# A recurrence and a highway layer on one core: shared PSUM slots, 4 KB load runs and a new instruction list

## The chip, the cores and the metric

The kernel runs on one core of a Trainium2 chip. The metric is the device time in microseconds (us), the median of several runs. Names used below: PE is the matrix engine (TensorE), DVE is VectorE, ACT is ScalarE, POOL is GpSimd, and SP is the engine that here issues all large transfers. SBUF is the on-chip memory, PSUM the small memory (eight banks of 2 KB in each of 128 partitions) that PE writes its results to.

## The reference

Two stages, one after the other. A gated recurrence runs over 6336 steps for 4 sequences with 256 channels, and then a highway layer is applied to each of the 25344 results:

```python
# x, f_logit: (4, 6336, 256); lower_bound: (256,)
sig = 1 / (1 + exp(-f_logit))
f = lower_bound + (1 - lower_bound) * sig
for t in range(S):
    h = f[:, t] * h + (1 - f[:, t]) * x[:, t]
    y[:, t] = h
# highway layer, w_h and w_t: (256, 256)
H = maximum(y @ w_h, 0)
T = 1 / (1 + exp(-(y @ w_t + b_t)))
out = T * H + (1 - T) * y
```

The types outside are float32. In all, 51.9 MB are read as x and f_logit and 25.95 MB are written.

## The kernel before

The tokens are cut into 24 units of 1024 tokens (8 blocks of 128, all of one sequence) and one last unit that holds the remaining 192 tokens of each of the 4 sequences (8 blocks of 96). The work on a unit before and in the recurrence is called its front, the highway layer its back. The first three units have their fronts cut into pieces, and the last unit has both cut in two, so there are 30 front pieces and 26 back pieces. Tokens lie on partitions when they are loaded; PE transposes them, so that the recurrence runs along the free dimension, with channels on partitions, as one scan instruction on VectorE for each half of the 256 channels.

Each step has a letter:

- L, X: load f_logit (tile lt) and x (tile xt) of a piece. Q: load the weights.
- U: ScalarE, u = sigmoid(-f_logit). P: GpSimd, bv = u * x for two blocks.
- A: PE transposes u into PSUM (uT). F: ScalarE, f = 1 - (1 - lb) * u out of uT.
- B: PE transposes bv into PSUM (bT). S: VectorE, the scan y out of f and bT.
- G, Z: PE, the two products with the weights (gp and zp), from y.
- T: ScalarE, t = sigmoid(zp + b). D: VectorE, d from y and gp (the ReLU and the subtraction of y in one instruction).
- E, H: e = d * t, the first part of the columns on VectorE (E) and the rest on GpSimd (H).
- O: PE, op = y + e, transposed back to tokens, four blocks in one PSUM tile. C, V: copy op to SBUF on ScalarE (C) or VectorE (V). R: store.

A string of letters gives the order in which all of these are put into the program. Each engine serves its own instructions strictly in that order.

```python
BUFS = dict(lt=5, xt=5, o=8, u=4, bv=2, f=6, t=2, d=2, e=2, y=7)
...
def load(i, name, src):
    u, j0, j1 = fronts[i]
    np_ = units[u][0]
    t = fs[i][name] = new(name, [NB, D], FP32)
    pin(nc.sync.dma_start(pairs(t[:np_, :j1 - j0]), tokens(src, u, j0, j1, 2)))   # runs of 2 tokens = 2 KB
...
def gpsimd_mul(out_, a, b):
    ins = pin(nc.gpsimd.tensor_mul(out_, a, b))
    while port:                     # GpSimd waits for the last e of VectorE that stands before it
        tc.add_manual_dep(ins.ins, port.pop().ins.name, ...)
...
def psum(piece, m, s, key, dtype):
    t = ps1.tile([P, NB * P], dtype, tag=key, name=key)     # one slot for each of uT, bT, zp, gp
    for c, h in enumerate(halves(piece)[m]):
        s[key, h] = t[:, c * 512:c * 512 + width(piece)]
        yield s[key, h], h
...
def scan(i, h):
    ...
        pin(nc.vector.tensor_tensor_scan(y, fs[i]["f", h][:, c:c + w], fs[i]["bT", h][:, c:c + w],
                                         0.0 if prev is None else prev, op0=ALU.mult, op1=ALU.add))
...
SHARE = 448                         # columns of e, for each half, that GpSimd takes
...
def e_dve(j):
    port.append(pin(nc.vector.tensor_mul(*e_cols(j, 0, width(backs[j]) - shared(j)))))
def e_pool(j):
    gpsimd_mul(*e_cols(j, width(backs[j]) - shared(j), width(backs[j])))

QB = NB // 2
def o_pe(j, q):
    op = bs[j]["op", q] = ps1.tile([P, QB, D], FP32, tag="op", name="op")       # one slot for op
    ...
            pin(nc.tensor.matmul(o, y[:, h, cols], diag[:, h], start=True, stop=False))
            pin(nc.tensor.matmul(o, bs[j]["e"][:, h, cols], ident_b, start=False, stop=True))

def copied(j, q):                   # in the last three pieces (HELPED) ScalarE and VectorE share the copy
    g = min(QB, shape(backs[j])[1] - q * QB)
    return g, g // 2 if j >= len(backs) - HELPED else g
...
PLAN = (
    "XLLXLXQQLXUUAPFFBAPSSUFFBASSWLLXLXPFFUPBAPFFUUPWSSLLXXLXPPGABZPPFFTDSSGABZUFFTDSSEAGBZFUFUTHPPPPPPDS"
    ... [cut] ...
    "OGFCTAOESDPHPPUCBZGOSDFTCBAZGORRRXRRRRXPHPUFTCSDEBAGZOSDFFTCABZGOFTCPPHRRRSSDEZGOBTFCRDGOZHSDDESCROT"
    "TCEVRGZOTTCDDVROEVCROCVR"
)
for k in PLAN:
    kinds[k][0](*next(todo[k]))
```

The PSUM slots before: uT and bT one bank each, zp, gp and op two banks each, one slot for each name, eight banks in all.

Of the kernel before, what the change touches and what calls it, by code (L numbers as in the profile page):

```python
# [19 lines left out]
def kernel(  # L20
# [43 lines left out]

    HELPED = 3

    first = ctx.enter_context(tc.tile_pool(name="first", bufs=1))
# [14 lines left out]
    def pin(ins):  # L84
        return tc.keep_in_program_order(ins)

    def pairs(t):

        return t.rearrange("p (k j) d -> p k (j d)", j=2)

    def inner(t):

        return t.rearrange("p k d j -> p k j d")
# [1 line left out]
    def tokens(src, u, j0, j1, j):  # L95

        np_, _, b, per, a = units[u]
        if per == NB:
            return src[b, a + j0 * np_:a + j1 * np_, :].rearrange("(k p j) d -> p k (j d)", p=np_, j=j)
        return src[b + j0 // per:b + j1 // per, a:a + per * np_, :].rearrange("b (p j) d -> p b (j d)", j=per)  # L100

    def load(i, name, src):
        u, j0, j1 = fronts[i]
        np_ = units[u][0]
        t = fs[i][name] = new(name, [NB, D], FP32)
        pin(nc.sync.dma_start(pairs(t[:np_, :j1 - j0]), tokens(src, u, j0, j1, 2)))

    def shape(piece):

# [43 lines left out]
    def gpsimd_mul(out_, a, b):  # L153

        ins = pin(nc.gpsimd.tensor_mul(out_, a, b))  # L155
        while port:
            tc.add_manual_dep(ins.ins, port.pop().ins.name, mybir.DependencyInfo(
                mybir.DependencyClass.Sync, mybir.DependencyReason.DATA), reason="shared port")

    def product(i, k):  # L160
        np_, _ = shape(fronts[i])
        if k == 0:
            fs[i]["bv"] = new("bv", [NB // 2, D, 2], BF16)
        gpsimd_mul(inner(fs[i]["bv"][:np_, k:k + 1])[:, 0], fs[i]["u"][:np_, 2 * k:2 * k + 2],
                   fs[i]["xt"][:np_, 2 * k:2 * k + 2])

    def width(piece):
        np_, nb = shape(piece)
# [3 lines left out]

        return ((0,), (1,)) if width(piece) > 512 else ((0, 1),)

    def psum(piece, m, s, key, dtype):

        t = ps1.tile([P, NB * P], dtype, tag=key, name=key)
        for c, h in enumerate(halves(piece)[m]):
            s[key, h] = t[:, c * 512:c * 512 + width(piece)]
            yield s[key, h], h  # L180

    def decay_pe(i, m):
        np_, nb = shape(fronts[i])
        for uT, h in psum(fronts[i], m, fs[i], "uT", FP16):
            for j in range(nb):
                pin(nc.tensor.transpose(uT[:, j * np_:(j + 1) * np_], fs[i]["u"][:np_, j, h * P:(h + 1) * P],  # L186
                                        ident_h[:np_, :np_]))

    def decay_act(i, h):

        np_, N = shape(fronts[i])[0], width(fronts[i])
        f = fs[i]["f", h] = new("f", [NB * P], FP16)
        pin(nc.scalar.activation(f[:, :N].rearrange("p (k q j) -> p k q j", q=np_, j=2),  # L193
                                 fs[i]["uT", h].rearrange("p (k j q) -> p k q j", q=np_, j=2), AF.Identity,
                                 scale=ncc[:, h:h + 1], bias=1.0))

    def b_pe(i, m):
        np_, nb = shape(fronts[i])
        for bT, h in psum(fronts[i], m, fs[i], "bT", BF16):

            for k in range(nb // 2):
                pin(nc.tensor.transpose(bT[:, 2 * k * np_:2 * (k + 1) * np_].bitcast(FP32),  # L202
                                        fs[i]["bv"][:np_, k, h * P:(h + 1) * P].rearrange("p d j -> p (d j)").bitcast(FP32),
                                        ident_f[:np_, :np_]))

# [17 lines left out]
        u, j0, j1 = backs[j]  # L223
        return ys[u][:, :, j0 * units[u][0]:j1 * units[u][0]]

    def ffn_pe(j, m, key, k):
        N = width(backs[j])
        for p, h in psum(backs[j], m, bs[j], key, FP32):
            for ki in range(NH):
                for a in range(0, N, 512):  # L230
                    e = min(a + 512, N)
                    pin(nc.tensor.matmul(p[:, a:e], w_sb[:, k, ki, h * P:(h + 1) * P], y_of(j)[:, ki, a:e],  # L232
                                         start=ki == 0, stop=ki == NH - 1))
# [9 lines left out]
        pin(nc.vector.scalar_tensor_tensor(bs[j]["d"][:, m, :width(backs[j])], y_of(j)[:, m], ncc[:, m:m + 1],  # L243
                                           bs[j]["gp", m], op0=ALU.mult, op1=ALU.max))

    SHARE = 448

    def shared(j):

# [5 lines left out]
        return (bs[j][key][:, :, a:e] for key in "edt")  # L255

    def e_dve(j):
        port.append(pin(nc.vector.tensor_mul(*e_cols(j, 0, width(backs[j]) - shared(j)))))  # L258

    def e_pool(j):  # L260
        gpsimd_mul(*e_cols(j, width(backs[j]) - shared(j), width(backs[j])))

    QB = NB // 2

    def o_pe(j, q):

        op = bs[j]["op", q] = ps1.tile([P, QB, D], FP32, tag="op", name="op")
        (np_, nb), y = shape(backs[j]), y_of(j)
        j0, j1 = q * QB, min((q + 1) * QB, nb)
        g = min(j1 - j0, units[backs[j][0]][3])  # L270
        for k in range(j0, j1):
            b, i = divmod(k - j0, g)
            cols = slice((j0 + b * g) * np_ + i, (j0 + (b + 1) * g) * np_, g)
            for h in range(NH):
                o = op[:np_, k - j0, h * P:(h + 1) * P]
                pin(nc.tensor.matmul(o, y[:, h, cols], diag[:, h], start=True, stop=False))  # L276
                pin(nc.tensor.matmul(o, bs[j]["e"][:, h, cols], ident_b, start=False, stop=True))  # L277

    def copied(j, q):

        g = min(QB, shape(backs[j])[1] - q * QB)
        return g, g // 2 if j >= len(backs) - HELPED else g

    def o_copy(j, q, engine):
        np_ = shape(backs[j])[0]
        if ("o", q) not in bs[j]:
            bs[j]["o", q] = new("o", [QB, D], FP32)
        g, a = copied(j, q)
        part = slice(0, a) if engine is nc.scalar else slice(a, g)
        copy = nc.scalar.copy if engine is nc.scalar else nc.vector.tensor_copy  # L290
        pin(copy(bs[j]["o", q][:np_, part], bs[j]["op", q][:np_, part]))  # L291

    def store(j, q):
        u, j0, _ = backs[j]
        a, (g, _) = j0 + q * QB, copied(j, q)
        per = min(g, units[u][3])
        pin(nc.sync.dma_start(tokens(out_bsd, u, a, a + g, per),
                              bs[j]["o", q][:units[u][0], :g].rearrange("p (k j) d -> p k (j d)", j=per)))

    def each(pieces, count):  # L300
        return [(i, k) for i, piece in enumerate(pieces) for k in range(count(piece))]

    def groups(piece):
        return -(-shape(piece)[1] // QB)


    kinds = {
# [1 line left out]
        "X": (lambda i, _: load(i, "xt", x), each(fronts, lambda p: 1)),  # L309
        "Q": (lambda i, k: load_weights(k), [(0, 0), (0, 1)]),  # L310
        "U": (lambda i, _: gate(i), each(fronts, lambda p: 1)),
        "P": (product, each(fronts, lambda p: shape(p)[1] // 2)),
        "A": (decay_pe, each(fronts, lambda p: len(halves(p)))),
        "F": (decay_act, each(fronts, lambda p: NH)),
        "B": (b_pe, each(fronts, lambda p: len(halves(p)))),
        "S": (scan, each(fronts, lambda p: NH)),
        "W": (lambda i, h: weights(h), [(0, 0), (0, 1)]),
        "Z": (lambda j, m: ffn_pe(j, m, "zp", 1), each(backs, lambda p: len(halves(p)))),
        "T": (t_act, each(backs, lambda p: NH)),
        "G": (lambda j, m: ffn_pe(j, m, "gp", 0), each(backs, lambda p: len(halves(p)))),  # L320
        "D": (d_dve, each(backs, lambda p: NH)),
        "E": (lambda j, _: e_dve(j), each(backs, lambda p: 1)),
        "H": (lambda j, _: e_pool(j), [(j, 0) for j in range(len(backs)) if shared(j)]),
        "O": (o_pe, each(backs, groups)),
        "C": (lambda j, q: o_copy(j, q, nc.scalar), each(backs, groups)),
        "V": (lambda j, q: o_copy(j, q, nc.vector), [p for p in each(backs, groups) if p[0] >= len(backs) - HELPED]),
        "R": (store, each(backs, groups)),
    }

    PLAN = (  # L330
        "XLLXLXQQLXUUAPFFBAPSSUFFBASSWLLXLXPFFUPBAPFFUUPWSSLLXXLXPPGABZPPFFTDSSGABZUFFTDSSEAGBZFUFUTHPPPPPPDS"
        "SOGABZCFTDSSAOGHPPPPFABZDSUFCTGBZALLXLXXLLRUTUFDSBGEESDOZBAGCTUFSDPPPPHZOBASTCFGZOBAPPPPHTCFDSZGOABD"
        "ESTUCFGZOABTFCDZAGOHPPPPFTCSDEEAGBOZXXRRLRRRRLLXFUCTDSAGBOZDSPHPPPFCTAOBZGESDFCOBATUFPPPPHPPZGATFCSD"
        "BZGAOTFCUSDPPHBZGAOXRRXXLRXLRRRTFCSDEBGAZOFTCESDABZGOPPPPPPHFTUCSDABGZOSEDPPHFTCABZGOFTUCSDRRXLLXRRR"
        "XBZGAOSDTFCBAGOZPHPPPPSDEFUTCBAGZOSDFTCABZGOPPHPPSDEFTCXLLRRRRBGAOZESDUFCTBOAGZSPHPPPPPPUFTCBADSGZOB"
        "FTCDESAGOZBHPPPPUCFTDSOGAZBCTFDSOGZBAHPCTUFDEESGZOABXRRRXRLLXLLRRDSTFCPPPPPHZGAOBTFCDSZGOBAUTCDSPPPH"
        "ZGODEFTCUBZAGOFTCESDABZGOFTCUSDPPHPPHPPPABZGOSDRXRRLRRRLXTCFBZOAGSEDTCFBZAGOTUCFSDBZGOAPPPPPHTCSDEZB"
        "OGFCTAOESDPHPPUCBZGOSDFTCBAZGORRRXRRRRXPHPUFTCSDEBAGZOSDFFTCABZGOFTCPPHRRRSSDEZGOBTFCRDGOZHSDDESCROT"
        "TCEVRGZOTTCDDVROEVCROCVR"
    )  # L340
    assert all(PLAN.count(k) == len(places) for k, (_, places) in kinds.items())
    todo = {k: iter(places) for k, (_, places) in kinds.items()}
    for k in PLAN:
        kinds[k][0](*next(todo[k]))
# [1 line left out]
_INS = ['x', 'f_logit', 'lower_bound', 'moe_w_h', 'moe_w_t', 'moe_b_t']  # L346
_OUTS = [((25344, 256), 'float32')]
# [25 lines left out]
```

## Time and profile before

| | |
|---|---|
| time, median of 3 runs | 219.93 us (219.38 to 220.0) |
| span of the profiled run | 219.6 us |
| a scan of 1024 columns (S), VectorE | 2340 ns, x40 |
| d (D), 1024 columns, VectorE | 1259 ns, x48 |
| e (E), 1152 elements, VectorE | 839 ns mean, x24 |
| e (H), 896 elements, GpSimd | 1911 ns, x24 |
| bv (P), 512 elements, GpSimd | 1173 ns, x96 |
| f, t, o copy (F, T, C), 1024 columns, ScalarE | 1176, 1165, 1060 ns |
| u (U), 2048 elements, ScalarE | 1955 ns, x21 |
| bytes moved | 78.68 MB, mean 358 GB/s over the span |

A page of the profile begins with the busy time of each engine and its share of the span. The durations of one instruction in the table overlap a little with the next one on the same engine, so the time from start to start in the timeline is shorter (2.26 us for a scan that is shown with 2.34). The chain that ended last follows the run back from its last instruction, at each step to what released it. A wait is listed with the engine and tile that waited, what it waited for, the total in us, the number of times and the longest.

### The profile page before, as it was taken

To read this page: it belongs to the slowest core of one execution; us is meant where nothing else is said; L and a number is where in the kernel's file an instruction comes from. 1 tells how busy PE (TensorE), PEld (TensorE's weight loads), DVE (VectorE), ACT (ScalarE), POOL (GpSimd) and SP (SyncE) were. 2 spreads that over 40 slices of the span, in tenths; PEclk is the share of its full clock that TensorE was granted. 3 is DMA by queue.
4 is the path that set the end of the run, shared out by engine and by line. 5 is a ranking of instruction groups with operands and counts; after the bars stand their busy time and mean duration, and the time that the engine had idled before them with its cause. 6 is when DMAs were issued, how large, how long until landed. Compare 5 with 4: busy or idle time off the path is not lost.

```text
span 219.6 us, 4569 instructions
## 1 busy us (share of the span) xinstructions
PE 188.4 (86%) x1772; PEld 132.9 (61%) x1800; DVE 197.2 (90%) x154; ACT 195.4 (89%) x194; POOL 161.1 (73%) x136
## 2 busy tenths in 40 slices
PE   0578787799999999999998999999999969998840
PEld 0435554466776766776766677566767656766640
DVE  1488978999999999999999999999999997999931
ACT  3679999999999999999999999999999958987621
POOL 4758579699769697889986979599687769663200
PEclk9999999999999999999999999999999997999975
DMA  5999999999999999999999999999999992644553
GB/s 146 401 408 408 411 403 408 409 404 409 405 416 415 403 414 404 411 417 409 409 410 407 402 418 416 409 408 406 416 413 413 349 357 112 215 169 168 212 213 103
DMA packets 34741, 78.68 MB, mean 358 GB/s; under 512 B 2336, under 2 KB 2848, under 8 KB 34720
## 3 DMA queue, kind: packets, MB, share of 16 engines
q1 hardware_dynamic: 34176, 78.39, 92.1%
q8 instruction: 14, 0.23, 0.4%
q10 hardware_dynamic: 544, 0.00, 0.1%
q14 instruction: 7, 0.06, 0.1%
HBM read 52.43 MB, written 25.95 MB: 357 GB/s over the span
## 4 chain that ended last, share of the span: by engine, by line
PE 29%; DVE 25%; DMA 15%; ACT 14%; issue 9%; POOL 4%; SPq 1%; DVEq 0%; POOLq 0%; ACTq 0%
DVE y L217 13%; PE gp L232 9%; DMA xt<-in_x_dram 9%; DVE d L243 8%; PE zp L232 6%; DMA lt<-in_f_logit_dram 5%; ACT t L238 5%; ACT f L193 4%; ACT o L291 4%; PE bT L202 4%; PE op L276 4%; PE op L277 3%; PE uT L186 3%; POOL bv L155 3%; DVE e L258 2%
## 5 line engine op out<-in xcount | busy, mean ns | idle before, releaser
L155 POOL TENSOR_TENSOR bv<-u,xt 128x512 bf16<-128x512 f16 (+1 forms) x100 | 114.3, 1173 | 30.8 <-DVE e L258 8.7
L217 DVE TENSOR_TENSOR_SCAN y<-f,y,bT 128x1024 bf16<-128x1024 f16 (+3 forms) x56 | 106.7, 1919 | 2.1 <-PE bT L202 2.0
L243 DVE SCALAR_TENSOR_TENSOR d<-y,ncc,gp 128x1024 bf16<-128x1024 bf16 (+1 forms) x52 | 62.7, 1209 | 3.0 <-PE gp L232 2.9
L193 ACT ACTIVATE f<-uT,ncc 128x1024 f16<-128x1024 f16 (+3 forms) x60 | 59.7, 1007 | 2.3 <-PE uT L186 2.3
L291 ACT COPY o<-op 128x1024 f32<-128x1024 f32 (+2 forms) x50 | 51.1, 1021 | 10.8 <-PE op L277 8.1
L238 ACT ACTIVATE t<-zp,bt 128x1024 bf16<-128x1024 f32 (+1 forms) x52 | 58.0, 1120 | 1.9 <-PE zp L232 1.0
L232 PEld LDWEIGHTS <-w_sb 128*128 128x128 f16 x400 | 38.2, 99 | 35.3 <-issue 4.4
L276 PE MATMUL op<-diag,y 128*128 128x128 f16 (+1 forms) x400 | 51.6, 222 | 3.5 <-ACT o L291 1.8
L155 POOL TENSOR_TENSOR e<-d,t 128x896 bf16<-128x896 bf16 x24 | 45.9, 1911 | 11.8 <-DVE e L258 5.0
L232 PE MATMUL gp<-y,w_sb 128*128 128x512 bf16 (+1 forms) x189 | 51.8, 387 | 2.9 <-DVE d L243 1.5
L277 PE MATMUL op<-ident_b,e 128*128 128x128 bf16 (+1 forms) x400 | 51.6, 222 | 2.5 <-POOL e L155 2.2
L149 ACT ACTIVATE u<-lt 128x2048 f16<-128x2048 f32 (+3 forms) x30 | 49.6, 1657 | 3.3 <-DMA lt<-in_f_logit_dram 3.1
L277 PEld LDWEIGHTS <-e 128*128 128x128 bf16 (+1 forms) x400 | 45.5, 116 | 10.6 <-issue 3.3
L232 PE MATMUL zp<-y,w_sb 128*128 128x512 bf16 (+1 forms) x183 | 49.5, 377 | 0.9
L276 PEld LDWEIGHTS <-y 128*128 128x128 bf16 (+1 forms) x400 | 45.7, 116 | 3.9
L186 PE MATMUL uT<-ident_h,u 128*128 128x128 f16 (+1 forms) x400 | 32.5, 227 | 8.6 <-ACT u L149 6.8
L202 PE MATMUL bT<-ident_f,bv 128*128 128x128 f32 (+1 forms) x200 | 32.4, 284 | 7.5 <-DVE y L217 5.9
L186 PEld LDWEIGHTS <-u 128*128 128x128 f16 (+1 forms) x400 | 27.5, 102 | 16.6 <-ACT u L149 8.2
L202 PEld LDWEIGHTS bT<-ident_f,bv 128*128 128x128 f32 (+1 forms) x200 | 22.0, 144 | 14.9 <-issue 5.5
L258 DVE TENSOR_TENSOR e<-d,t 128x1152 bf16<-128x1152 bf16 (+1 forms) x26 | 20.7, 817 | 0.5 <-ACT t L238 0.5
L217 DVE TENSOR_TENSOR_SCAN y<-f,bT 128x512 bf16<-128x512 f16 (+2 forms) x8 | 10.5, 1341 | 3.6 <-PE bT L202 3.6
L291 DVE COPY o<-op 128x512 f32<-128x512 f32 (+1 forms) x4 | 2.8, 690 | 4.8 <-DMA out_dram<-o 3.2
(19 smaller groups left out, 7.5 us busy)
## 6 DMA issues: line engine op xcount, KB each, us to landing
out_dram<-o SPq DMA_DIRECT2D x48, 512.0 KB, 11.4
lt<-in_f_logit_dram SPq DMA_DIRECT2D x21, 1024.0 KB, 13.9
xt<-in_x_dram SPq DMA_DIRECT2D x21, 1024.0 KB, 13.9
lt<-in_f_logit_dram SPq DMA_DIRECT2D x5, 512.0 KB, 8.0
xt<-in_x_dram SPq DMA_DIRECT2D x5, 512.0 KB, 9.1
lt<-in_f_logit_dram SPq DMA_DIRECT2D x2, 384.0 KB, 11.4
xt<-in_x_dram SPq DMA_DIRECT2D x2, 384.0 KB, 5.4
out_dram<-o SPq DMA_DIRECT2D x2, 384.0 KB, 3.0
```

Of the source, the lines that this page charges most:

```text
L149: pin(nc.scalar.activation(u[:np_, :nb], fs[i]["lt"][:np_, :nb], AF.Sigmoid, scale=-1.0))
L155: ins = pin(nc.gpsimd.tensor_mul(out_, a, b))
L186: pin(nc.tensor.transpose(uT[:, j * np_:(j + 1) * np_], fs[i]["u"][:np_, j, h * P:(h + 1) * P], ident_h[:np_, :np_]))
L193: pin(nc.scalar.activation(f[:, :N].rearrange("p (k q j) -> p k q j", q=np_, j=2), fs[i]["uT", h].rearrange("p (k j q) -> p k q j", q=np_, ...
L202: pin(nc.tensor.transpose(bT[:, 2 * k * np_:2 * (k + 1) * np_].bitcast(FP32), fs[i]["bv"][:np_, k, h * P:(h + 1) * P].rearrange("p d j -> ...
L217: pin(nc.vector.tensor_tensor_scan(y, fs[i]["f", h][:, c:c + w], fs[i]["bT", h][:, c:c + w], 0.0 if prev is None else prev, op0=ALU.mult, ...
L232: pin(nc.tensor.matmul(p[:, a:e], w_sb[:, k, ki, h * P:(h + 1) * P], y_of(j)[:, ki, a:e], start=ki == 0, stop=ki == NH - 1))
L238: pin(nc.scalar.activation(bs[j]["t"][:, m, :width(backs[j])], bs[j]["zp", m], AF.Sigmoid, bias=bt[:, m:m + 1]))
L243: pin(nc.vector.scalar_tensor_tensor(bs[j]["d"][:, m, :width(backs[j])], y_of(j)[:, m], ncc[:, m:m + 1], bs[j]["gp", m], op0=ALU.mult, op1 ...
L276: pin(nc.tensor.matmul(o, y[:, h, cols], diag[:, h], start=True, stop=False))
L277: pin(nc.tensor.matmul(o, bs[j]["e"][:, h, cols], ident_b, start=False, stop=True))
L291: pin(copy(bs[j]["o", q][:np_, part], bs[j]["op", q][:np_, part]))
```

## The change

Five things change together.

1. PSUM slots are no longer tied to a product. There are two slots of one bank ("one0", "one1"), used by uT and bT, and three slots of two banks ("two0" to "two2"), used by zp, gp and op. The list names the slot by a digit behind each of A, B, Z, G and O. The eight banks stay the same. This lets one product have two or three slots where it is needed.
2. The loads fetch four tokens of a partition in one run of 4 KB instead of two in 2 KB. The order of tokens within a block changes, so F reads uT with four in place of two interleaved blocks, and B writes bT with a step of two words.
3. Two products of the first unit (EARLY) run on VectorE instead of GpSimd.
4. The last piece's output is copied and stored in groups of two blocks (LASTQ), one copied on ScalarE and one on VectorE, in place of one group of four that both share.
5. GpSimd's share of e rises from 448 to 512 columns for each half, and the list is new. In it x is loaded right after f_logit of the same piece, both gp halves of a unit can be filled together at the start, and the last output groups go to different slots.

```diff
+    LASTQ = 2
+    EARLY = [(0, 0), (2, 0)]
 ...
     def load(i, name, src):
         u, j0, j1 = fronts[i]
-        np_ = units[u][0]
+        np_, j = units[u][0], run(fronts[i])
         t = fs[i][name] = new(name, [NB, D], FP32)
-        pin(nc.sync.dma_start(pairs(t[:np_, :j1 - j0]), tokens(src, u, j0, j1, 2)))
+        pin(nc.sync.dma_start(t[:np_, :j1 - j0].rearrange("p (k j) d -> p k (j d)", j=j), tokens(src, u, j0, j1, j)))
+
+    def run(piece):
+        u, j0, j1 = piece
+        return min(4, j1 - j0, units[u][3])
 ...
+    def vector_mul(out_, a, b):
+        port.append(pin(nc.vector.tensor_mul(out_, a, b)))
 ...
-    def psum(piece, m, s, key, dtype):
-        t = ps1.tile([P, NB * P], dtype, tag=key, name=key)
+    def psum(slot, shape, key, dtype):
+        tag = ("one" if dtype in (FP16, BF16) else "two") + slot
+        return ps1.tile([P, *shape], dtype, tag=tag, name=key)
 ...
-    def b_pe(i, m):
-        np_, nb = shape(fronts[i])
-        for bT, h in psum(fronts[i], m, fs[i], "bT", BF16):
+    def b_pe(i, m, slot):
+        (np_, nb), r = shape(fronts[i]), run(fronts[i]) // 2
+        for bT, h in filled(fronts[i], m, slot, fs[i], "bT", BF16):
+            t = bT.bitcast(FP32).rearrange("p (k j q) -> p k j q", q=np_, j=r)
             for k in range(nb // 2):
-                pin(nc.tensor.transpose(bT[:, 2 * k * np_:2 * (k + 1) * np_].bitcast(FP32),
+                pin(nc.tensor.transpose(t[:, k // r, k % r],
 ...
-    SHARE = 448
+    SHARE = 512
 ...
+    def group(j, q):
+        size = LASTQ if j == len(backs) - 1 else QB
+        g = min(size, shape(backs[j])[1] - q * size)
+        if j < len(backs) - HELPED:
+            return q * size, g, g
+        return q * size, g, g // 2 if size == QB else (g if q % 2 == 0 else 0)
 ...
     PLAN = (
-        "XLLXLXQQLXUUAPFFBAPSSUFFBASSWLLXLXPFFUPBAPFFUUPWSSLLXXLXPPGABZPPFFTDSSGABZUFFTDSSEAGBZFUFUTHPPPPPPDS"
+        "LLXXLXQQUUA0pFFB1PSLXLXLXLSA0B1UFFpSSWWA0PFFUXLXLB1PSA0PSUFFUPPG0G1Z2B1DDSZ0STTA0B1PPHEFFUPSXXLA0SPF"
 ... [cut] ...
-        "TCEVRGZOTTCDDVROEVCROCVR"
+        "PCCFDSERG0G1RDSHZ2Z0B1DFTTSZ2G1O0HTTSDDCO2G1EERDO0CDO2CVRO1RCVZ0RCVTRTEO2O1CVRR"
     )
-    for k in PLAN:
-        kinds[k][0](*next(todo[k]))
+    letters = iter(PLAN)
+    for k in letters:
+        kinds[k][0](*next(todo[k]), *([next(letters)] if k in "ABZGO" else []))
```

## The prediction, as it was put on record before the changed kernel was run

> **What bounds the kernel now.** I read the page's totals and slices first, then the stage windows, the chain that ended last, and the timelines of single engines at the two ends.
>
> ```profile
> PE 188.4 (86%) x1772; PEld 132.9 (61%) x1800; DVE 197.2 (90%) x154; ACT 195.4 (89%) x194; POOL 161.1 (73%) x136
> ...
> GB/s 146 401 408 408 411 403 408 409 404 409 405 416 415 403 414 404 411 417 409 409 410 407 402 418 416 409 408 406 416 413 413 349 357 112 215 169 168 212 213 103
> ```
>
> VectorE, ScalarE and the DMA queue are all near their limit; the transfers run at about 410 GB/s until 181 us (33 slices of 5.5 us) and at about half of that afterwards. The windows say where engines are idle (columns: length, then busy us of PE, weight loads, DVE, ACT, POOL, then granted clock, DMA share, GB/s):
>
> ```profile
> 0.00:20.00 20.00, 10.54 (x63) 6.70 (x64) 10.95 (x17) 13.32 (x20) 11.87 (x21) 1.00 0.93 334
> 20.00:40.00 20.00, 15.36 (x126) 9.81 (x128) 17.62 (x15) 19.79 (x19) 16.11 (x14) 1.00 1.05 407
> 40.00:60.00 20.00, 18.50 (x182) 13.37 (x186) 20.00 (x14) 19.92 (x19) 16.78 (x14) 1.00 1.05 406
> ...
> 180.00:200.00 20.00, 19.15 (x179) 13.66 (x183) 18.77 (x16) 16.71 (x19) 13.78 (x11) 0.91 0.45 169
> 200.00:219.60 19.60, 10.84 (x120) 8.48 (x118) 10.39 (x17) 7.57 (x12) 1.89 (x1) 0.79 0.47 175
> ```
>
> From 40 to 180 us VectorE and ScalarE do not rest. The scans of 1024 columns start at 42.14 us and, 35 scans later, at 174.10 us in VectorE's timeline: 3.77 us each, 7.54 us for a unit (two scans at 2.26 us from start to start, two d at 1.17, one e at 0.67). VectorE's idle time is 219.6 - 197.2 = 22.4 us: 11.4 before 40 us, 10.4 after 180, under 1 between. So there is nearly nothing to win in the middle without removing work, and some 20 us of idle time at the ends, of which part (first load, last store) must stay.
>
> At the start the products wait for data; at the end one PSUM slot serves all output groups. From the list of waits, and the end of the chain (start us, us, what):
>
> ```profile
> POOL bv L155 <- DMA xt<-in_x_dram: 6.8, 5, 1.8
> DVE y L217 <- PE bT L202: 5.7, 5, 2.3
> ```
> ```profile
> 205.09 0.22 PE op L276
> 206.20 0.59 ACT o L291
> 206.82 0.70 DVE o L291
> 207.56 0.22 PE op L276
> 208.66 0.59 ACT o L291
> 209.27 0.70 DVE o L291
> 210.02 0.22 PE op L276
> 211.11 0.70 DVE o L291
> 211.83 0.59 ACT o L291
> 212.44 2.54 DMA out_dram<-o
> 214.97 0.69 DVE o L291
> ```
>
> The last four groups go strictly one after another, about 2.5 us each: fill the slot, copy one half on one engine, the other half on the other, fill again. The piece called a DMA is really the next fill and ScalarE's copy: ScalarE's timeline has that copy at 214.36, waiting for PE, and VectorE's at once after it.
>
> **What the Trainium skill says.** "Perfetto Trace Analysis", Optimizing Tensor Performance, says independent matmul groups should rotate through PSUM banks so that the evacuation of one overlaps the next; the chain above is the case where they do not, the middle (PE 19 us busy of 20) the case where one slot per product was enough. "SBUF — State Buffer", two separate sides, says that VectorE with two SBUF inputs and GpSimd lock one shared port pair for a whole instruction. The trace agrees: e has a median of 752 ns but a longest of 2425 ns. "DMA: Bandwidth & Descriptors", Specifications, puts the fabric's ceiling at 435 GB/s; the loads of 2 KB runs already reach 410 here, so 4 KB runs can gain at most 6%.
>
> **The change part by part.**
>
> *The e split.* GpSimd's share goes from 448 to 512 columns per half, VectorE's e from 1152 elements to 1024. e of 768 elements took 554 ns, of 1152 752 ns: 0.52 ns an element, 66 ns a unit, 1.6 us over 24 units. GpSimd's part costs 1.84 us for 896 elements from start to start, so 2.10 for 1024: 6.3 us more in all, minus two products at 1.14. GpSimd then needs 4 x 1.14 + 2.10 = 6.66 us a unit, plus 0.6 in which it stands aside for e: 7.3 of 7.54 us. It fits, barely. ScalarE's work, 195.4 us, is untouched, and so are the 78.4 MB. A unit moves 3.15 MB, which at 410 GB/s takes 7.67 us, more than VectorE's 7.54 today. I credit the middle with 0.7 of the 1.6 us.
>
> *The start.* In the new list x follows f_logit piece by piece; in the old one f_logit runs up to two pieces ahead. Bytes queued ahead of the x of unit 2's second half fall from 8.9 to 6.8 MB, 5.1 us at 408 GB/s. I walked both lists with the durations above. First product: on VectorE some 0.6 us after its data instead of 1.17 on GpSimd, and f_logit is fetched first, 0.45 us earlier, so the first scan comes at 6.9 us instead of 7.86. That lead is lost: the next VectorE product waits for the third x piece (about 9.2 us), and both lists then wait for the weights, so the scan of the third piece stays at 12.7 us. After that both halves of gp are filled at once (two slots), and unit 1's scans come at the old times, with e earlier. A stall of 1.3 us appears at 23.6 us, where PE stands at the first output group until GpSimd's first e, with the next bT behind it. Unit 2's scans no longer wait for x: unit 3's first scan starts at 32.7 us in my walk, against 35.1. By then one e more and one d less has been done (worth 0.5 us), so the lead is 1.9 us; port collisions of e with products can take some. I credit 1.7 us.
>
> *The end.* After the second scan of unit 22 (it ended at 187.9 us) VectorE had 17.2 us to the end of unit 23's e at 205.1, with almost no idle time. The new order leaves one more e there: 17.8 us, and I add 1 us for stalls of a new order. From that e to the end of the run took 14.5 us. Now the groups have three slots, so I sum: two output fills of PE 1.8, the third 0.9, copy on ScalarE 0.58, two sigmoids 1.06, e 0.5, last fill 0.9 to 1.8 at the low clock, VectorE's copy 0.7: 7.4 us. The last store stays: 219.6 - 215.7 = 3.9. Sum 11.3, a gain of 3.2, less 1.6 for the extra e and the stalls. The half-sized groups let the first store of the last piece leave early, but the second still ends the run.
>
> *Stalls before the end.* At 177.5 us two e in a row took 3.27 instead of 1.4 us (GpSimd held the port), and the scan at 185.6 waited 1.15 us. The new list never has two e of 1024 in a row after the start. I credit 2.2 of these 3.0 us.
>
> Sum: 0.7 + 1.7 + 3.2 - 1.6 + 2.2 = 6.2 us, so 219.9 - 6.2 = 213.7; I say 213.5.
>
> **The rivals.** (a) *PE becomes the bound.* It serves its list in order and needs about 7.0 us of the 7.54 (16 products of 512 columns at 0.216, 32 output products at 0.056, 16 transposes at 0.056, 8 at 0.11). The new list still refills the same bT slot for both scans of a unit, and puts an output group behind that fill; if PE then stands over 0.5 us a unit, VectorE starves. My walk has it standing 0.65 us there, caught up later in the unit. If it does not catch up, 0.2 us a unit for 20 units is 4 us: about 217.5. The strided write of bT (every second word) could add to PE; nothing in the trace speaks to it. (b) *GpSimd becomes the bound.* 7.3 us plus semaphore latency is near 7.54; e then waits for the port in each unit. At 7.7 us a unit the time would be 213.5 + 22 x 0.16 = 217. For it: the 2425 ns e. Against: GpSimd is now 73% busy. (c) *DMA becomes the bound.* If the rate stays 410 GB/s, compute can only use up the lead; the middle gives nothing and the result is 214.5. If 4 KB runs raise it to 420, the start gains too: 212.
>
> **Range and chances.** The gains at the two ends rest on visible waits, and the losses on close fits, so the range leans upward: 209.5 to 218.5. Faster by over 2% means under 215.5, some 2 us above my figure, where one rival in full or two in part would put it: 0.68. Slower by over 2%, above 224.3, needs a stall in every unit of half a microsecond or more: 0.06. The rest, 0.26, is within 2%.
>
> **What would show it.** Right: VectorE's idle time falls to about 16 us, mostly in the windows before 40 and after 180 us; the scan period stays between 7.45 and 7.6 us; the copies of the last groups overlap fills; the wait for x shrinks from 6.8 us. Wrong: VectorE below 19.5 of 20 us in the middle with waits on bT or gp (rival a), e with a median well above 0.75 us (rival b), or the products waiting for x after 45 us (rival c).

## The result and the profile after

The changed kernel takes 214.25 us (median of 4 runs, 213.96 to 214.44), the kernel before 219.66 us on the same chip (4 runs, 219.16 to 220.0). The ratio is 0.9754, with an interval of 0.9729 to 0.9779: 5.4 us less. The prediction was 213.5 us.

One line of the diff that is printed above has to be read differently: in the kernel that ran, B arranges bT with `"p (k q j) -> p k j q"`, not `"p (k j q) -> p k j q"`. That is the step of two words which the text above it names.

First the page of the changed kernel: total busy time of each engine, then the transfer rate in 40 slices of 5.3 us.

```profile
PE 185.4 (87%) x1773; PEld 130.9 (62%) x1800; DVE 196.1 (92%) x156; ACT 194.2 (91%) x194; POOL 164.8 (78%) x134
...
GB/s 152 406 419 420 422 417 420 423 415 417 419 418 422 415 417 422 416 422 417 418 419 417 421 415 421 419 413 422 416 412 362 369 305 314 167 178 293 5 352 192
```

VectorE is busy almost as long as before (197.2 us there), in a shorter span: it is idle for 212.5 - 196.1 = 16.4 us instead of 22.4. The rate has risen from about 410 to about 418 GB/s. The stage windows of the changed kernel (columns as in the prediction) show where the idle time went:

```profile
0.00:20.00 20.00, 10.35 (x59) 6.47 (x60) 13.14 (x20) 12.82 (x19) 11.08 (x20) 1.00 0.90 345
20.00:40.00 20.00, 15.58 (x152) 11.14 (x155) 16.96 (x15) 18.75 (x20) 17.39 (x14) 1.00 1.02 420
40.00:60.00 20.00, 18.39 (x172) 12.65 (x173) 20.00 (x13) 20.00 (x20) 18.30 (x15) 1.00 1.03 418
...
180.00:200.00 20.00, 19.62 (x185) 13.28 (x186) 20.00 (x21) 17.34 (x22) 11.91 (x8) 1.00 0.47 180
200.00:212.50 12.50, 6.08 (x87) 5.11 (x85) 6.68 (x12) 5.29 (x8) 0.53 (x1) 0.89 0.62 232
```

After 180 us VectorE is idle for 5.8 us, before it was 10.4. In the first 20 us its idle time falls from 9.05 to 6.86 us, but 1.46 of these 2.2 us are the two products (0.73 us each) that it now does itself; between 20 and 40 us it is idle longer than before (3.04 against 2.38 us). So the page itself says that the gain lies at the end and not at the start.

To place it, I cut both traces at events of VectorE that mean the same work. "4th scan" is the start of the fourth scan of 1024 columns; by then both kernels have done seven d and three e.

| stretch | before, us | after, us | gain, us | remark |
|---|---|---|---|---|
| start to 4th scan | 45.57 | 46.39 | -0.82 | |
| to second scan of unit 21 | 128.53 | 128.34 | +0.19 | after does one more e here |
| to second scan of unit 22 | 11.47 | 6.87 | +4.60 | before does two e here, after none |
| to the end of unit 23's e | 19.51 | 20.15 | -0.64 | after does one more e and two more short scans here |
| to the end of the span | 14.52 | 10.75 | +3.77 | before does these two short scans here |
| sum | 219.60 | 212.50 | +7.10 | |

An e takes 0.67 us before and 0.60 after, two short scans (192 columns each, of the last unit) 1.0 us. For equal work the middle gains 0.8 us, the third stretch 4.60 - 1.34 = 3.3, the fourth 1.0 and the last 2.7. Both traces of the kernel before are of longer runs (221.41 us here and 221.82 in the second, with medians of 219.66 and 220.84 us), so the sum exceeds 5.4 us, and what a shorter run loses at each place is not shown. In the second trace (further below) the third stretch takes 11.99 us, and the last two together 33.22 us instead of 34.03.

The end of the changed kernel, in VectorE's timeline (start us, us, line, operation; in brackets the idle time before it and what ended it):

```profile
203.67 0.69 DVE L303 COPY o<-op 128x512 f32<-128x512 f32 x1 [0.30 <-ACT o L303]
204.55 0.69 DVE L303 COPY o<-op 128x512 f32<-128x512 f32 x1 [0.20 <-ACT o L303]
...
206.61 0.56 DVE L166 TENSOR_TENSOR e<-d,t 128x768 bf16<-128x768 bf16 x1 [0.48 <-ACT t L251]
208.30 0.69 DVE L303 COPY o<-op 96x512 f32<-96x512 f32 x1 [1.13 <-PE op L297]
```

The copies of the last full groups now follow each other at 0.88 us, where the chain of the kernel before showed 2.5 us for each group. After them come ScalarE's sigmoid, the last e, one fill and one copy.

### The profile page after: what moved, and what is told of

Same layout as the page of the kernel before. It is cut to its first block, busy times and chain, and to the rows that moved or that the text cites. A ratio compares the mean times of both kernels' runs of the same rounds, so it can differ in the third digit from the quotient of the medians.

```text
span 212.5 us, 4575 instructions
## 1 busy us (share of the span) xinstructions
PE 185.4 (87%) x1773; PEld 130.9 (62%) x1800; DVE 196.1 (92%) x156; ACT 194.2 (91%) x194; POOL 164.8 (78%) x134
## 3 DMA queue, kind: packets, MB, share of 16 engines
q1 hardware_dynamic: 22160, 78.39, 92.7%
## 4 chain that ended last, share of the span: by engine, by line
PE 40%; ACT 27%; DMA 13%; DVE 12%; issue 6%; SPq 1%; ACTq 0%; DVEq 0%
DMA lt<-in_f_logit_dram 11%; PE gp L245 10%; PE zp L245 9%; ACT f L205 9%; ACT t L251 9%; ACT u L154 7%; PE op L296 6%; DVE y L230 6%; PE op L297 6%; PE bT L215 5%; PE uT L198 5%; DVE d L256 4%; ACT o L303 3%; DMA xt<-in_x_dram 2%; DVE e L166 1%
## 5 line engine op out<-in xcount | busy, mean ns | idle before, releaser
L160 POOL TENSOR_TENSOR bv<-u,xt 128x512 bf16<-128x512 f16 (+1 forms) x98 | 111.9, 1174 | 26.5 <-DVE e L166 10.4
L205 ACT ACTIVATE f<-uT,ncc 128x1024 f16<-128x1024 f16 (+3 forms) x60 | 67.4, 1143 | 1.1 <-PE uT L198 1.1
L251 ACT ACTIVATE t<-zp,bt 128x1024 bf16<-128x1024 f32 (+1 forms) x52 | 61.3, 1278 | 1.3 <-PE zp L245 0.9
L154 ACT ACTIVATE u<-lt 128x2048 f16<-128x2048 f32 (+3 forms) x30 | 54.0, 1800 | 6.1 <-DMA lt<-in_f_logit_dram 5.8
L160 POOL TENSOR_TENSOR e<-d,t 128x1024 bf16<-128x1024 bf16 x24 | 51.6, 2149 | 8.7 <-DVE e L166 7.4
L303 ACT COPY o<-op 128x1024 f32<-128x1024 f32 (+2 forms) x50 | 54.1, 1187 | 4.5 <-PE op L297 4.5
L297 PE MATMUL op<-ident_b,e 128*128 128x128 bf16 (+1 forms) x400 | 49.5, 219 | 2.9 <-DVE e L166 1.7
L245 PE MATMUL gp<-y,w_sb 128*128 128x512 bf16 (+1 forms) x178 | 48.8, 380 | 1.8 <-DVE d L256 0.8
L296 PE MATMUL op<-diag,y 128*128 128x128 f16 (+1 forms) x400 | 49.6, 219 | 0.8 <-ACT t L251 0.7
L166 DVE TENSOR_TENSOR e<-d,t 128x1024 bf16<-128x1024 bf16 (+1 forms) x26 | 18.7, 723 | 2.1 <-ACT t L251 2.0
```

The lines of the kernel that those rows point to most:

```text
L154: pin(nc.scalar.activation(u[:np_, :nb], fs[i]["lt"][:np_, :nb], AF.Sigmoid, scale=-1.0))
L251: pin(nc.scalar.activation(bs[j]["t"][:, m, :width(backs[j])], bs[j]["zp", m], AF.Sigmoid, bias=bt[:, m:m + 1]))
L303: pin(copy(bs[j]["o", q][:np_, a:e], bs[j]["op", q][:np_, a:e]))
```

## The experiments

Twelve runs were made, in three sets; two of them repeat the two kernels unchanged. Each set has its own runs of the kernel before on the same chip (medians 220.84, 220.97 and 220.44 us), so I compare ratios to the kernel before; a difference of 0.01 is 2.2 us. Where a capital letter is named, it is that of the list (S scan, D, E and H the two parts of e, P product, O fill of an output group, C copy, R store).

### One slot for the last output groups

In the changed kernel, the last groups all go to one slot again, in an order that allows it. Nothing else changes.

```diff
-DO0CDO2CVRO1RCVZ0RCVTRTEO2O1CVRR
+DO0CDCVO0RRCVO0Z1RCVTRTEO0CO0VRR
```

> The changed kernel with its last five output groups all in one PSUM slot, in the same order on every engine. Theory E: fills and copies go one after another again, some 2.5 us for a full group, worked out at 3.0 us more: 217.2 us (216.5 to 218). Rival O (it is the order of the last units, not the slots): under 1 us more, below 215.2.

Ratio 0.9959 (0.9936 to 0.9982), against 0.9754 for the changed kernel: 4.5 us of the 5.4 are lost. VectorE's timeline:

```profile
206.96 0.69 DVE L303 COPY o<-op 128x512 f32<-128x512 f32 x1 [1.76 <-ACT o L303]
210.10 0.69 DVE L303 COPY o<-op 96x512 f32<-96x512 f32 x1 [2.45 <-ACT o L303]
...
214.42 0.69 DVE L303 COPY o<-op 96x512 f32<-96x512 f32 x1 [1.96 <-PE op L297]
```

From unit 23's e (it starts at 202.00 us here, at 201.16 in the changed kernel) to the last copy it takes 12.4 us, in the changed kernel 7.1: 5.3 us in one trace, from the slots alone, where 3.0 were expected. With the copy before them, which starts at 204.50 us, the first two lines give spacings of 2.46 and 3.14 us, where the changed kernel has 0.88. The second is the longer one because PE is slow there: one output product takes 0.11 us at 208 us, where the changed kernel has 0.06 us at 204 us. The granted clock of this run falls in its last two slices:

```profile
PEclk9999699999999999999999999999999999999966
```

So the serial end costs twice in this trace: the waits, and a longer fill while the granted clock is lower. The second part is an association; no run changed the clock alone.

### The last piece in groups of four blocks (LASTQ = 4)

```diff
-    LASTQ = 2
+    LASTQ = 4
...
-TEO2O1CVRR
+TEO2CVR
```

> The changed kernel with the last piece as one group of four blocks, copied half by ScalarE and half by VectorE, and one store. Theory E: the fill is one of 0.9 us instead of two of 0.45 and the two copies of one tile follow each other, so 0.4 us later at the copy and up to 0.3 us more for the larger store: 214.6 to 215.1. Rival: no difference, 214.0 to 214.5, because the second small store ends the run anyway.

Ratio 0.9786 (0.974 to 0.9831): 0.7 us more than the changed kernel, within the uncertainty. VectorE's last copy starts at 209.35 us after a wait of 1.75 us for ScalarE's, since the two again share one group. From the second scan of unit 22 to the end the trace takes 31.98 us, that of the changed kernel 30.90. The small groups are worth about a microsecond, if anything.

### 2 KB load runs in the changed kernel

```diff
-        return min(4, j1 - j0, units[u][3])
+        return min(2, j1 - j0, units[u][3])
```

> The changed kernel with runs of 2 KB again in the loads. Theory E (the gain sits in the last 40 us, in PSUM slots and order; the transfers are not the bound): 214.6 to 215.4 us, that is 0.4 to 1.1 more than the changed kernel's 214.25, because early f_logit pieces arrive some 2% later. Rival K (4 KB runs make the gain by the higher rate): 217 to 219, most of the 5.4 us lost, with the rate in the middle back at 410 GB/s and engines waiting for loads after 45 us.

Ratio 0.9801 (0.9755 to 0.9847), about 1.0 us more, and the intervals overlap. The windows show the lower rate, while VectorE and ScalarE stay near 20 of 20 us:

```profile
80.00:100.00 20.00, 19.46 (x189) 13.75 (x188) 19.79 (x15) 20.00 (x19) 18.02 (x14) 1.00 1.05 409
```

A unit takes 7.54 us with 2 KB runs and 7.53 with 4 KB (the mean of 35 scans from the fourth on). So rival (c), DMA as the bound of the middle, is out: the rate moved by 2% and the pace didn't follow. Most of what is lost lies before the middle: the first VectorE product starts at 7.34 us (6.07 in the changed kernel's trace) and the fourth scan at 47.85 (46.39 there; 46.80 and 47.12 in the two runs above, which have the same start). Another 0.6 us lies after unit 22's second scan (31.51 us to the end, 30.90 in the changed kernel).

### GpSimd's share of e back to 448

```diff
-    SHARE = 512
+    SHARE = 448
```

> The changed kernel with GpSimd's share of e back at 448 columns, VectorE's at 1152 elements. Theory A (ScalarE sets the pace of the middle, at 7.57 us a unit against VectorE's 7.46): at most 0.5 us more, scan period 7.53 to 7.57. Rival D (VectorE sets it): the whole 1.6 us more, period 7.60 or above. A third possibility, GpSimd's port lock: 0.5 to 1 us less, with shorter e.

Ratio 0.9741 (0.9703 to 0.978); the changed kernel, run again in the same set, has 0.9752 (0.9713 to 0.9791). VectorE's e in the changed kernel, then here (min/median/max in ns):

```profile
L166 DVE TENSOR_TENSOR e<-d,t x26: 557/684/1402, 20.3 to 206.6; 128x1024 bf16<-128x1024 bf16 x24, 128x768 bf16<-128x768 bf16 x2
```
```profile
L166 DVE TENSOR_TENSOR e<-d,t x26: 557/750/947, 22.1 to 208.1; 128x1152 bf16<-128x1152 bf16 x24, 128x768 bf16<-128x768 bf16 x2
```

The median goes from 684 ns to 750 ns, 24 times, and the time does not move; a unit takes 7.54 us against 7.53. Making VectorE's part shorter is worth nothing here. The run of the changed kernel in this set had this expectation:

> The changed kernel once more, as the yardstick of this set. Ratio to the kernel before 0.9754 as at first, 0.973 to 0.978; about 214 to 215.5 us.

Its span was 213.4 us, with the last copy at 209.25 us; it is what the later kernels of the second and third set are held against.

Why nothing? ScalarE's timeline of the changed kernel from one u to the next:

```profile
47.53 2.00 ACT L154 ACTIVATE u<-lt 128x2048 f16<-128x2048 f32 x1
49.33 2.01 ACT L303 COPY o<-op 128x1024 f32<-128x1024 f32 x2
51.12 1.23 ACT L205 ACTIVATE f<-uT,ncc 128x1024 f16<-128x1024 f16 x1
52.13 2.23 ACT L251 ACTIVATE t<-zp,bt 128x1024 bf16<-128x1024 f32 x2
54.12 1.24 ACT L205 ACTIVATE f<-uT,ncc 128x1024 f16<-128x1024 f16 x1
55.12 2.05 ACT L154 ACTIVATE u<-lt 128x2048 f16<-128x2048 f32 x1
```

There is no gap, and a unit takes 7.59 us (the next u follows at 62.71): 1.80 for u, four times 1.00 for f and t, two copies of 0.90, all from start to start. VectorE's own work for a unit is shorter: two scans of 2.26 us, two d of 1.17 and an e of 0.60 are 7.46 us, and 7.53 with the old share (an e of 0.67). Yet a unit takes 7.53 to 7.54 us with both, so what VectorE saves comes back as short waits. That ScalarE sets the pace is read from these timelines; no run shortened ScalarE's work.

### The kernel before again, with the stall at 177 us

No edit. The question was whether the stall of two e in a row recurs.

> The kernel before, unchanged, for a second trace. If the stalls at 177 to 186 us (two e in 3.3 us instead of 1.4, a scan that waits 1.15 us) belong to its list, they come again within half a microsecond, in a span of about 218 us; if they came from the lower PE clock of that one trace, the stretch from 174.1 to 185.6 us shrinks by 1.5 us or more.

One run, 221.82 us. It recurs. GpSimd's timeline, then VectorE's:

```profile
177.88 1.17 POOL L155 TENSOR_TENSOR bv<-u,xt 128x512 bf16<-128x512 f16 x1 [2.81 <-DMA xt<-in_x_dram]
179.00 2.40 POOL L155 TENSOR_TENSOR e<-d,t 128x896 bf16<-128x896 bf16 x1
```
```profile
178.22 3.79 DVE L258 TENSOR_TENSOR e<-d,t 128x1152 bf16<-128x1152 bf16 x2
```

GpSimd's first product of unit 23 waits 2.81 us for an x load. In the trace of the kernel before, that load was issued at 165.21 us, and landed 11.3 us later. GpSimd serves its list in order, so its part of e, which needs nothing of that load, stands behind the product. When it comes at last, it falls on VectorE's own pair of e, which takes 3.79 us instead of 1.4. PE's next output group needs GpSimd's e, and behind it in PE's list stand the gp and bT that VectorE's next d and scan need.

PE then loses time of its own. It stands idle for 1.43 us until GpSimd's e, and from 182 to 184 us its granted clock is 0.50 in both traces of the kernel before. PE's timeline of the first one shows the gp behind that wait:

```profile
181.14 1.91 PE L232 MATMUL gp<-y,w_sb 128*128 128x512 bf16 x4
```

In the next two runs, where the clock stays at 1.00, these four products take 1.03 us.

### GpSimd's e ahead of that product, in the kernel before

One letter of the list moves, H ahead of one P.

```diff
-GOAPPPPPHTC
+GOAPPPPHPTC
```

> The kernel before with one swap in its list: GpSimd's e of unit 19 stands ahead of the first product of unit 23 instead of behind it. Theory X (that product waits to 176.6 us for an x piece that was sent late behind stores, and e of GpSimd, VectorE's next e, PE's output group and the next gp all queue up behind it): the stretch from the scan at 174.1 us to the one at 185.6 us falls from 11.5 to about 8.6 us, and 2 to 3 us of it reach the end: ratio 0.986 to 0.991. Rival: VectorE is behind anyway and loses the same time later: ratio above 0.996.

Ratio 0.9899 (0.985 to 0.9949): 2.2 us less, from one letter. VectorE's timeline:

```profile
178.40 1.56 DVE L258 TENSOR_TENSOR e<-d,t 128x1152 bf16<-128x1152 bf16 x2
...
183.32 2.33 DVE L217 TENSOR_TENSOR_SCAN y<-f,y,bT 128x1024 bf16<-128x1024 f16 x1
```

The pair of e takes 1.56 us and the second scan of unit 22 starts 8.35 us after that of unit 21, instead of 11.47 (11.99 in the second trace of the kernel before). This shows the queue order as the cause: with two e in a row still there, and the load as late (the product that waits for it starts at 177.51 us, 177.88 in the trace above), the stall is gone.

### 4 KB load runs alone, in the kernel before

Loads, F and the order of the transposes as in the change; list and slots as before. In this kernel bT is written without the step of two words, so within each group of four tokens u·x meets the f of another token. Bytes, instructions and their sizes are those of 4 KB runs, so its time can be read, but it isn't the same function.

> The kernel before with 4 KB runs in the loads, nothing else. Theory E: the rate in the middle rises from 410 to 418 GB/s and the middle stays the same, since ScalarE and VectorE set its pace; the start gains some half a microsecond and the late x piece of unit 23 comes a little earlier: ratio 0.992 to 0.999. Rival K (the runs make the gain): below 0.985.

Ratio 0.9899 (0.9847 to 0.9952), 2.2 us less, more than my theory had. VectorE's timeline says why:

```profile
178.82 1.41 DVE L264 TENSOR_TENSOR e<-d,t 128x1152 bf16<-128x1152 bf16 x2
```

From the second scan of unit 21 (175.39) to that of unit 22 it takes 8.20 us: with a faster queue the x load is there in time, GpSimd's products run on without a gap, and the same stall is gone. So 4 KB runs alone, one letter alone, and the new list each remove this one stall. They can't be added: inside the changed kernel, 4 KB runs are worth only the 1.0 us above.

### Other orders of the start and the end

I tried to get more out of the two ends of the changed kernel. None of the four is faster than it.

The start: u of unit 4 moved behind t and f of the units before, so that VectorE's e doesn't wait for t (see the next section for that wait).

```diff
-UO1B0O2LLXXA1PSSPCCFFUPG0G1B0PPPDSSDZ2Z0A1A0TTFFEZ2B1Z0A0TTUFG1G2SDDB1HPPPPHPO0
+UB0O1O2LLXXA1PSSPCCFFPG0G1B0PDSSDZ2Z0A1A0TTEHFFUZ2B1Z0TTG1G2A0FUSDDB1PPPPPPHPO0
```

> The changed kernel with a new order from 22 to 40 us only: u of unit 4 after t of unit 1 and f of unit 3, the second GpSimd e before the products of unit 4, and the sixth bT before the first output group. Theory: the order of ScalarE made unit 3 late (e waited for t behind a u that waited for f_logit), so unit 3's first scan comes at 32.3 instead of 35.1 us; as ScalarE then sets the pace, 1.2 to 2.0 us of it reach the end: ratio to the changed kernel 0.991 to 0.994. Rival: f_logit arriving late is the limit itself, whatever the order: within 0.4 us of the changed kernel.

Ratio 0.986 (0.9808 to 0.9911), 2.4 us slower than the changed kernel (five of its six runs lie between 218.2 and 218.8 us, one at 215.6). In the changed kernel of this set a scan waits 1.88 us behind the output groups in PE's list. They still stand ahead of gp, and the wait now comes ahead of d in VectorE's timeline:

```profile
30.72 1.28 DVE L256 SCALAR_TENSOR_TENSOR d<-y,ncc,gp 128x1024 bf16<-128x1024 bf16 x1 [2.21 <-PE gp L245]
```

Unit 3's first scan starts at 36.88 us instead of 36.09, and GpSimd's e before it came after 4.80 us of idle time.

The end: earlier copies and stores, in two versions. First a small one:

```diff
-DDCO2G1EERDO0CDO2CVRO1RCVZ0RCVTRTEO2O1CVRR
+DDCO2G1Z0EERDCO2DO1TTCVERO0CVRRO2O1CVRCVRR
```

> The changed kernel with the last piece's zp filled, and its t and e done, before the copies of the groups ahead of it, and the slots of the last groups turned accordingly. Theory: the last t stands behind three copies and their fills on ScalarE; taken out, VectorE's last copy ends 2.0 us earlier than 209.0: 1.3 to 2.2 us less in all. Rival: the stores of the last 3 us queue up and the end stays within 0.5 us.

Ratio 0.976 (0.9717 to 0.9803), no change. Then one that also lets unit 22's stores leave earlier, so that the queue is free for the last ones:

```diff
-Z2Z0B1DFTTSZ2G1O0HTTSDDCO2G1EERDO0CDO2CVRO1RCVZ0RCVTRTEO2O1CVRR
+Z2Z0B1DFTTSO2O0G1HCCZ2STTDDRRG1Z0EEDO2DO1TTCVERO0CVRO2O1CVRCVRR
```

> The changed kernel with the last piece's t and e taken ahead of the copies, as in the run where the end did not move, and in addition both output groups of unit 22 filled and copied before the t of the last piece but one, so that their two stores leave at about 200 instead of 202 to 203 us. Theory S (in that run the stores of the last 8 us queued up): the last store now has a free queue and the run ends 3.5 us after VectorE's last copy, 1.3 to 2.5 us less than the changed kernel: ratio to the kernel before 0.964 to 0.969. Rival: fills and copies of unit 22 delay the last piece by as much: within 0.5 us of the changed kernel.

Ratio 0.9757 (0.9699 to 0.9814), again no change. VectorE's last copy ends at 208.56 us, 1.4 us sooner than in the changed kernel of the set before (209.25 + 0.69), and the span is 213.7 us against 213.4. The windows of the last microseconds of this kernel:

```profile
208.00:210.00 2.00, 0.00 (x0) 0.00 (x0) 0.56 (x1) 0.00 (x0) 0.00 (x0) 1.00 1.00 369
210.00:212.00 2.00, 0.00 (x0) 0.00 (x0) 0.00 (x0) 0.00 (x0) 0.00 (x0) 0.60 0.97 310
```

And of the changed kernel:

```profile
208.00:210.00 2.00, 0.27 (x5) 0.12 (x3) 0.69 (x1) 0.44 (x1) 0.00 (x0) 0.92 0.83 259
210.00:212.50 2.50, 0.00 (x0) 0.00 (x0) 0.00 (x0) 0.00 (x0) 0.00 (x0) 0.50 0.25 84
```

The columns before the last are the clock and the DMA share. Work that ends sooner hands its stores over all at once: in the reordered kernel the issues of the last five stores, together 1.79 MB, begin between 206.1 and 209.0 us, and the DMA engines are full (shares 1.00 and 0.97) from 208 to 212. In the changed kernel of the set before, the same five are spread from 205.3 to 210.0 us; its shares are 0.97 and then 0.65 (0.83 and 0.25 in the trace shown), so the queue drains soon after the last store is issued. The end has passed from the slots to the stores: this is read from the windows, and no run changed the stores alone.

Last, the end of that kernel together with a milder start:

```diff
-CCFFUPG0G1B0PPPDSSDZ2Z0A1A0TTFFEZ2B1Z0A0TTUFG1G2SDD
+CCFFPG0G1B0PDSSDZ2Z0A1A0TTEFFUPPZ2B1Z0TTG1G2A0UFSDD
```

> The kernel with the new end of the run before this one, and in addition only u of unit 4 behind t of unit 1 and f of unit 3, its first two products behind that e, and the sixth uT slot user behind gp of unit 2; the first output group stays where the changed kernel has it. Theory: unit 3's first scan comes 1 to 2.5 us earlier, and as ScalarE saves the wait of 1.25 us for f_logit, 0.8 to 1.3 us reach the end. Rival: as in the first try, a later wait (gp, or uT of unit 4) takes it back: within 0.4 us of the run before, or slower.

Ratio 0.988 (0.9829 to 0.9931). The first scan of unit 3 does come earlier against unit 2's: 8.4 us after it (27.14 to 35.52), 9.6 in the changed kernel of the set before (26.52 to 36.09). But the products of unit 4 now wait 5.8 us for their u, and the cost comes out a few instructions later in VectorE's timeline:

```profile
44.71 2.35 DVE L230 TENSOR_TENSOR_SCAN y<-f,y,bT 128x1024 bf16<-128x1024 f16 x1 [1.68 <-PE bT L215]
```

An e right after it takes 2.11 us instead of 0.67. The fourth scan starts at 50.20 us, 2.9 later than in the kernel with the same end and the old start (47.28), and the span ends 3.1 later (216.8 against 213.7). The other pair, the first start order against the changed kernel, says the same: 2.6 us late at the fourth scan, 3.3 at the end. The middle makes up for nothing that is lost before it.

## Why the prediction was right or wrong

The total was near (213.5 against 214.25 us), but that is partly luck: a step that failed and steps that were too small cancel.

| step | predicted, us | measured in the traces, us |
|---|---|---|
| middle, e split | +0.7 | +0.2; +0.8 with the one more e done there |
| start | +1.7 | -0.8 |
| stalls before the end | +2.2 | +3.3 (4.6 less two e) |
| one e more and new stalls | -1.6 | -0.6: the e (0.6) and two short scans (1.0), less 1.0 saved |
| end | +3.2 | +3.8, of which 1.0 are the two scans done earlier |

**The start failed.** The step was "unit 3's first scan starts at 32.7 us in my walk, against 35.1". It starts at 35.14 us, before at 35.10. The other traces have the same sign: the fourth scan starts at 46.39 to 47.49 us in seven traces with the new start and 4 KB runs, at 45.57 to 46.38 in three with the old start. The walk was right in two places before that: third piece 12.74 us (walk 12.7), and a stall of 0.94 us before 24.64 (1.3 at 23.6). The first scan comes at 7.66 us, nearer to the old 7.86 than to the walk's 6.9. After 24.64 us the walk fails. VectorE's timeline of the changed kernel:

```profile
33.29 1.40 DVE L166 TENSOR_TENSOR e<-d,t 128x1024 bf16<-128x1024 bf16 x1 [1.53 <-ACT t L251]
35.14 2.29 DVE L230 TENSOR_TENSOR_SCAN y<-f,bT 128x1024 bf16<-128x1024 f16 x1 [0.45 <-PE bT L215]
```

and ScalarE's:

```profile
29.34 1.91 ACT L154 ACTIVATE u<-lt 128x2048 f16<-128x2048 f32 x1 [1.25 <-DMA lt<-in_f_logit_dram]
31.15 2.10 ACT L251 ACTIVATE t<-zp,bt 128x1024 bf16<-128x1024 f32 x2
```

The e waits for t, and t stands in ScalarE's list behind u of unit 4, which waits 1.25 us for its f_logit. The e itself then takes 1.40 us, while GpSimd's products run (31.87 to 34.14 us). The walk followed VectorE, GpSimd and PE and gave ScalarE no queue of its own. And it counted only one side of the loads' order: x comes earlier because f_logit comes later. The list of waits of the changed kernel:

```profile
ACT u L154 <- DMA lt<-in_f_logit_dram: 5.8, 5, 1.6
...
POOL bv L160 <- DMA xt<-in_x_dram: 4.1, 4, 1.9
```

Before, the products waited 6.8 us for x and u waited 3.1 us for f_logit. The waits for x shrank as predicted, by 2.7 us, and the waits for f_logit grew by the same 2.7. How these waits fall differs from trace to trace. From 21 us to unit 3's first scan VectorE waits for 2.9 us in the changed kernel's trace (0.94 for bT behind the output group, 1.53 for t, 0.45 for bT) and for 3.0 us in its second one (0.25 for f, 1.88 for bT, 0.16, 0.24 for t, 0.46 for bT). So the wait for t alone isn't the cause. The two runs that moved u took it away, and the milder one brought unit 3's first scan 1.2 us nearer to unit 2's, but both paid more elsewhere. What would have to move so that unit 3's first scan comes the 2.4 us earlier that the walk promised stays open. A loss at the start reaches the end, by what the last two pairs of runs show; that a gain would is not shown.

**Middle.** The size was right by luck, the reasoning wasn't. "0.52 ns an element" is right (684 against 750 ns), but the run with the old share shows it worth nothing: its trace takes 128.52 us for this stretch against 128.34, so only 0.2 of the 0.8 us can come from the split. The prediction took VectorE for what sets the pace; the trace has ScalarE without a gap. The period lies inside the 7.45 to 7.6 of the prediction only because it didn't move (over this stretch 7.55 us a unit, 7.56 before).

**Rivals.** (a) PE: VectorE is busy for 20.00 of 20 us between 40 and 60 us and for 39.80 of 40 from 60 to 100, and bT with its step of two words takes 282 ns against 284. (b) GpSimd: e has a median of 684 ns, and giving GpSimd less changes nothing. (c) DMA: out, by the 2 KB run.

**Stalls before the end.** The term was too small (2.2 against 3.3 us), and the cause was only half named. "Two e in a row" with GpSimd at the port is what the trace shows, and the Trainium skill, "SBUF — State Buffer", two separate sides, describes that lock for a whole instruction; the trace agrees in that the pair takes 1.4 us alone and 3.3 to 3.8 with GpSimd there. But the run with one letter moved leaves the two e in a row and loses the stall. What set it off is a late x load at the head of GpSimd's list, and PE's lower clock after the wait added to it.

**The extra e and new stalls.** From the end of unit 22's second scan (183.94 us) to the end of unit 23's e it takes 17.8 us, the figure of the prediction without its stalls, but by other terms: beside the e (0.6 us) the new list does two short scans (1.0 us) here that the sum left out, and 1.0 us is saved. The 1 us for stalls of a new order didn't occur: VectorE is busy 20.00 us of the 20 from 180 us.

**The end.** The sum of 11.3 us measured 10.75, and the idea is borne out by the run with one slot, which loses 4.5 us. That is more than the end gains against the kernel before, because the run's end is more serial than that kernel's: from the end of unit 23's e it takes 15.6 us with five fills in a row, against 14.5 us with four, two short scans included. Of the 3.8 us gained, 1.0 came from doing these scans earlier, which the prediction had not counted. The Trainium skill, "Perfetto Trace Analysis", Optimizing Tensor Performance, on rotating groups through banks, holds here with these numbers. The half-sized groups were given nothing in the sum; the run with LASTQ = 4 puts them at 0.7 us, uncertain.

As a cross-check from runs alone: slots 4.5 and the stall 2.2, less 0.8 at the start as the traces have it, is 5.9 us, against 5.4 measured. Each of the two runs has an uncertainty near 1 us, and the 4.5 us are against an end more serial than that of the kernel before, so the nearness proves little. The two early products on VectorE were not run alone.

## What to carry to other kernels

When several engines each serve a list in order, follow all of them, the one that only feeds included: an instruction that waits for a load holds up everything behind it on its engine, also what doesn't need the load, and moving one kind of load forward moves another back. Give the last outputs as many PSUM slots as the middle can spare; once they overlap, look at when their stores are issued, not when the last copy ends. Before taking work from an engine in the steady middle, look at start-to-start times of every engine there, since the one without gaps may be another.

## What the runs showed of the hardware

- Load runs of 4 KB instead of 2 KB raise the rate of the full queue from about 410 to 418 GB/s, with 22160 packets instead of 34176 on that queue.
- Durations of ScalarE can grow with no change of pace: f takes 1143 ns in the mean after the change and 1007 before, an output copy 1187 against 1021, while in both traces f follows at 1.0 us and a copy at 0.9 from start to start. The busy sums of the rows of f, t, u and the copies are together 18.4 us larger after the change, while ScalarE's busy time as a whole is 194.2 us against 195.4.
- A product of 512 elements takes 0.73 us on VectorE and 1.17 on GpSimd.
- The granted PE clock can halve for some microseconds within a run. It was 0.50 from 182 to 184 us in the stall of the kernel before, and 0.50 from 208 to 210 us with one slot, where PE was busy for all of the 2 us and an output product took 0.11 us instead of 0.06. In both cases PE had been busy for only about 0.6 of the 2 us some microseconds earlier (0.51 of 2 at 178 us, 0.60 of 2 at 206 us). That is no rule: in the changed kernel PE was busy for 0.83 of 2 us at 22 us, and the clock stayed at 1.00.
